# A fused attention and FFN kernel on one core: seven block products for the last pieces, and maxima sent through DRAM

## The chip, the cores and the metric

The kernel runs on one core of one Trainium2 chip. The metric is the device time of one execution in microseconds, 985.25 before the change (median of three runs, 983.32 to 985.38). TensorE (PE) multiplies, VectorE (DVE) and ScalarE (ACT) work element by element, GpSimd (POOL) clears memory here, and SyncE (SP) issues all transfers.

## The reference

`q`, `k` and `v` have 8 batches, 8 heads, 576 positions and 64 dimensions. Attention is causal by blocks of 64: a query sees every key of its own and of earlier blocks. The result, 4608 tokens of 512 numbers, goes through an FFN of 2048 hidden units:

```python
scores = scale * np.matmul(q, k.transpose(0, 1, 3, 2))     # scale = 1/8
scores = np.where(block_i >= block_j, scores, -1e9)
attn = softmax(scores)
x = (attn @ v), heads side by side                          # 4608 x 512
h = x @ w_in                                                # 512 x 2048
g = h * np.clip(h + 3.0, 0.0, 6.0) / 6.0
out = (g @ w_out).astype(np.float32)                        # 2048 x 512
```

## The kernel before

**Precision.** Most products are made of 16-bit numbers: each operand is scaled by a power of two and split into a high and a low half (`hi` and `lo`), and a product is three: hi·hi, hi·lo, lo·hi. The scale comes from the largest magnitude in the operand. For the weights it is taken by chunk of 256 hidden units (`NCH` = 8 chunks, `w_max`, line 678), for `v` by batch (`v_max`, 747). `pow2_scale` (561) turns maxima by partition, `mx`, into one maximum known to all 128 partitions. With `exact` it does so on TensorE: a product with the identity lays the 128 maxima side by side (`mt`), DVE reduces them, a second product with ones spreads the result (`mb`).

**Attention.** 32 slots, each a batch and a pair of heads (`n`). A slot's `q` and `k` are loaded, scaled and transposed by a DMA (`qk_load`, `qk_prep`, tile `qkT`). `s_group` (1035) makes scores (`s`), the softmax in `p` and the split `ph` or `phl`, which DMAs transpose into `pT`; `pv_group` (1157) multiplies by `v`, split by `v_prep` (761), and writes the slot's part of `x`, high and low half. The first four slots have versions in f32 (names with 32).

**The FFN.** The tokens are cut into 13 pieces (`pieces`, 1141): piece 0, 2 and 4 to 12 of 384 tokens, 1 and 3 of 192. Four buffers `xb` hold `x` of a piece by its number modulo 4. For each of 16 tiles of 128 hidden units, `f`, `ffn1_` (1246) makes `h` = 24 products of 64 hidden units by 384 tokens (4 depths of 128, 3 splits, 2 halves of the columns of the array, which run at the same time) in a PSUM tile `h`; then ScalarE makes `r` = relu(h + 3), DVE `r` = min(r, 6)·h, ScalarE or DVE the high half of `g`, DVE the low one. `ffn2_` (1302) accumulates `g` times `w_out` in three PSUM tiles `o`, 18 products of 512 columns for each `f`; after the last `f` they are scaled into tiles `osb` and stored. `g` has four buffers (`NGB`), `stage` (shared by `r`, `osb` and the preparation of weights) four, `raw` one.

**What sets the order.** Nothing is issued when it is written. The class `Recorder` (85) keeps every instruction with its tiles, a key (the time when it is wanted) and the engines that may do it (`scaled`, 150: "A", "V" or "P"). `schedule` (289) then plays the program on a model of the engines: whenever an engine is free it takes the ready instruction with the lowest key. Keys come from the times at the top: `AT` for the attention slots, `FT` for the pieces, `W0`, `S0`, `M0` for loads, splits and maxima of the weights; `ADV` makes TensorE's attention work earlier. A buffer is given out only if it doesn't block an instruction that stands earlier in the program (`room`, 335): where a tag has one buffer, an earlier user that hasn't begun holds back a later one. `QUEUE` (98) says when a transfer lands by the plan. The resulting order is emitted, instruction by instruction, each engine in its own fixed order; on the chip an engine waits for semaphores.

`ffn_step` (1361) gives the program order of the FFN: `ffn1` of the next tile, `ffn2` three tiles behind (`LAG`). `step` (1469) calls it at the piece's times once the piece's `x` is complete.

Of the kernel before, what the change touches and what calls it, by code (L numbers as in the profile page):

```python
# [24 lines left out]

U = 1.592
AS = (6.899, 12.918, 18.225, 24.115)
AL = 17.759
PV0 = 2.584
TA, TR, PR = 2.701, 5.502, 1.15  # L30
QR = 2.616
PVA, PVB = 1.013, 0.991
PHS = 18
# [4 lines left out]
EVR = 3  # L38
EVP = 4
PRO = True  # L40
MEM = 0

NMIN = 64
QL = -3.431
VL = -2.484
W0, WD = 16.803, 2.29
S0, SD = 55.334, 4.109
M0, MD = 36.221, 7.195
RT = (29.488, 39.58, 49.409, 59.423)
RS, RL, VL1 = 2.209, 24.843, 24.11  # L50
VM0, VMX = 49.529, 0.186
AT = ((4, 86.25), (6, 123.23), (8, 163.76), (9, 178.32), (10, 200.46), (12, 251.25), (14, 297.48), (15, 319.97), (16, 344.82), (24, 581.69), (32, 825.86))
FT = ((0, 34), (1, 120), (2, 165.28), (3, 233.86), (4, 274.28), (5, 355.06), (7, 504.5), (10, 755.22), (13, 989.58))
UNI = False
QP = 0.558
VP = 0.387
BLK = 64
# [23 lines left out]

ADV = {("tensor", "a"): 99.24}


class Recorder:
# [11 lines left out]
    LOADS = 95.0  # L97
    BIAS = {"vector": 250.0, "gpsimd": 500.0}
    EDGE = 0.0
    BURST, PATIENCE = 3, 4000.0  # L100

    def __init__(self, nc):
        self.nc = nc
        self.ops = []
        self.key = 0.0
        self.cls = ""
        self.joint = None
        self.adv = ADV
        for n in self.NAMES:
# [6 lines left out]
    def box(a):  # L116
        sz = mybir.dt.size(a.dtype)
# [58 lines left out]
    def add(self, ways):  # L176
# [318 lines left out]
def kernel(  # L495
# [50 lines left out]
    attp = ctx.enter_context(tc.tile_pool(name="att", bufs=2))  # L546
    ffp = ctx.enter_context(tc.tile_pool(name="ff", bufs=3))
    ps_s = ctx.enter_context(tc.tile_pool(name="ps_s", bufs=3, space=bass.MemoryType.PSUM))
    ps_h = ctx.enter_context(tc.tile_pool(name="ps_h", bufs=2, space=bass.MemoryType.PSUM))
# [10 lines left out]

    def pow2_scale(mx, n, nm, to=None, exact=False):
# [8 lines left out]
        if exact:  # L570
            pt_ = ps_s.tile([P, 512], F32, tag="s", name=f"mt_{nm}")
            nc.joint = "mt", nm
            for h in range(2):
                wide = mx[:, h % n:h % n + 1].to_broadcast([P, BLK])
                nc.tensor.matmul(pt_[h * BLK:(h + 1) * BLK, :P], wide, ident, start=True, stop=True)
            nc.joint = None
            dg = sm.tile([P, n + 1], F32, tag=f"dg{n}", name=f"dg_{nm}")
            nc.vector.tensor_reduce(dg[:, n:], pt_[:, :P], axis=AX.X, op=ALU.max)
            nc.vector.tensor_scalar_mul(dg[:, :n], ident[:, :(n - 1) * BLK + 1:BLK], dg[:, n:])
            mx = dg[:, :n]  # L580
        ps = ps_s.tile([P, 512], F32, tag="s", name=f"mb_{nm}")
        nc.joint = "mb", nm
        for h in range(2):
            nc.tensor.matmul(ps[h * BLK:(h + 1) * BLK, :n], ones[:, :BLK], mx, start=True, stop=True)
        nc.joint = None
        nc.vector.tensor_scalar_max(am, ps[:, :n], TINY)
# [52 lines left out]
    def w_load(w, c, half):  # L639
# [36 lines left out]
        )  # L676

    def w_max(c):

        acc = sm.tile([P, 2, 2], F32, tag="wacc", bufs=2, name=f"wacc{c}")  # L680
        for wi, w in enumerate("io"):
            for half in range(2):
                c32 = w_f32(w, c, half)
                ab = ffp.tile([P, WC], F32, tag="stage", bufs=NST_B, name=f"ab{w}{c}_{half}")
                ab = ab.rearrange("p (r l n) -> p r l n", r=c32.shape[1], l=2)
                nc.scalar.activation(ab, c32, AF.Abs, accum_out=acc[:, wi, half:half + 1])
        m = sm.tile([P, 2], F32, tag="wm", name=f"wm{c}")
        nc.vector.tensor_reduce(m, acc, axis=AX.X, op=ALU.max)
        pow2_scale(m, 2, f"w{c}", (pwio[:, c], rsio[:, c]), exact=True)

    def w_split(c):

        rs = rsio[:, c]
        for wi, w in enumerate("io"):
            for half in range(2):
                c32 = w_f32(w, c, half)
                part = w_part(w, c, half)
                hi, lo = (part[:, :, i].rearrange("p r (l n) -> p r l n", l=2) for i in range(2))
                nc.scaled(hi, c32, rs[:, wi:wi + 1], "AVP")
                nc.vector.scalar_tensor_tensor(  # L700
                    lo, c32, rs[:, wi:wi + 1], hi, op0=ALU.mult, op1=ALU.subtract
                )

# [43 lines left out]
    def v_max(n):  # L747
# [8 lines left out]
        if hp == NPAIR - 1:  # L756
            m1 = sm.tile([P, 1], F32, tag="vm1", name=f"vm1_{b}")
            nc.vector.tensor_reduce(m1, vmax[b], axis=AX.X, op=ALU.max)
            vscale[b] = pow2_scale(m1, 1, f"v{b}", exact=True)

# [11 lines left out]

    def h_scale(b):

        if b not in hs:
            t = sm.tile([P, NCH], F32, tag="sh", bufs=3, name=f"sh{b}")
# [3 lines left out]
            nc.vector.tensor_scalar_mul(t, t, C_H)  # L780
            hs[b] = t
        return hs[b]

# [373 lines left out]
    def pv_group(n, g):  # L1157
# [56 lines left out]
    gt = {}  # L1214
    acc = {}

    def spans(pc):
# [28 lines left out]
    def ffn1_(pc, f):  # L1246
        if pc == 0:
            return ffn1_f32(f)
        x, w, fc = xb[pc % 4], width(pc), f * P % NH
        ps = ps_h.tile([P, TP], F32, tag="h", name=f"h{pc}_{f}")  # L1250
# [51 lines left out]
    def ffn2_(pc, f):  # L1302
# [34 lines left out]
        for t, a in enumerate(acc.pop(pc)):  # L1337
            n, half = min(w - t * P, P), w - t * P < P
            o = ffp.tile([P, DM], F32, tag="stage", bufs=NST_B, name=f"osb{pc}_{t}")
            oc = o[:, :DM // 2] if half else o  # L1340
            ac = a[:, :DM // 2] if half else a
            nc.scaled(oc, ac, so[:, t:t + 1] if pc else 1.0 / 6.0, "AV")
            rows = out[row + t * P:row + t * P + n]
            if half:
# [183 lines left out]
```

## Time and profile before

| | before |
|---|---|
| median of 3 runs | 985.25 us (983.32 to 985.38) |
| the profiled execution | 982.83 us, span 981.0 |
| TensorE, matmul | busy 964.2 us (98%) |
| VectorE | 756.4 us (77%) |
| ScalarE | 696.5 us (71%) |
| granted TensorE clock | 0.999 |

The span runs from the first to the last instruction; the execution's time has 1.8 us more. In the profile, an instruction is named by engine, operation and tiles: `h<-x,win` is a product that writes tile `h`. All of them stand under line 491, where the planner emits, so tiles tell them apart. "<-" behind a time names what ended the wait. A product of one half of the array's columns is written 128*64.

### The profile page before, as it was taken

The page shows a single profiled execution, that of the slowest core. Times are in us where ns is not written, and L with a number is a line of the kernel's source. Part 1 is how long each engine was busy: PE and PEld are TensorE (multiplying, and loading weights), DVE is VectorE, ACT ScalarE, POOL GpSimd, SP SyncE. Part 2 cuts the span into 40 slices and gives each one's busy share as a digit, 9 for nine tenths or more (in the row PEclk, how much of TensorE's full clock was granted, in tenths as well). Part 3 has the DMA queues.
Part 4 walks back from the last instruction along what each step waited for, and adds up shares of the span by engine and source line. Part 5 has one row for each costly group of instructions (what it writes and reads, how often), then busy time and mean ns, then how long its engine had stood idle before and what let it go on. Part 6 is the DMA issues. An engine that isn't in the chain of part 4 may idle for free.

```text
span 981.0 us, 29087 instructions
## 1 busy us (share of the span) xinstructions
PE 964.2 (98%) x11754; PEld 722.9 (74%) x11754; DVE 756.4 (77%) x2081; ACT 696.5 (71%) x1840; POOL 28.3 (3%) x109
## 2 busy tenths in 40 slices
PE   8999999999999999999999999999999999999998
PEld 6655447877778867777777677777777777777776
DVE  6889998999989999999999898899886432332331
ACT  6899789778778888888878788787775433333332
POOL 3012000000000000000000000000000000000000
PEclk9999999999999999999999999999999999999999
DMA  6966689899898899898899898786664200000000
GB/s 141 277 204 223 159 154 178 169 183 189 155 173 148 149 175 157 170 162 148 161 186 177 151 188 156 132 164 131 108 133 77 36 34 1 1 33 1 34 2 33
DMA packets 414199, 128.91 MB, mean 131 GB/s; under 512 B 403184, under 2 KB 403440, under 8 KB 414064
## 3 DMA queue, kind: packets, MB, share of 16 engines
q1 hardware_dynamic: 414064, 127.05, 66.5%
q8 instruction: 92, 1.51, 0.6%
q14 instruction: 43, 0.35, 0.1%
HBM read 45.09 MB, written 9.44 MB: 56 GB/s over the span
## 4 chain that ended last, share of the span: by engine, by line
PE 58%; DVE 6%; DMA 2%; ACT 1%; issue 1%; DVEq 0%; ACTq 0%
PE o L491 25%; PE h L491 25%; PE s L491 4%; PE pv L491 4%; DMA pT<-ph 2%; DVE st L491 1%; DVE phl L491 1%; DVE ph L491 1%; DVE r L491 1%; DVE g L491 1%; DVE qks L491 1%; DVE vhl L491 0%; ACT p L491 0%; DVE x L491 0%; ACT r L491 0%
## 5 line engine op out<-in xcount | busy, mean ns | idle before, releaser
L491 PE MATMUL h<-x,win 128*64 128x384 f16 (+3 forms) x4790 | 440.7, 319 | 4.4 <-DVE r L491 4.4
L491 PE MATMUL o<-wout,g 128*64 128x512 f16 (+2 forms) x3424 | 432.3, 383 | 0.0
L491 PEld LDWEIGHTS <-win 128*64 128x64 f16 x4608 | 296.1, 110 | 62.5 <-issue 6.5
L491 PEld LDWEIGHTS <-g 128*64 128x64 f16 x3264 | 219.2, 110 | 91.6
L491 ACT ACTIVATE r<-h,eg,sh 128x192 f32<-128x192 f32 (+1 forms) x240 | 134.1, 580 | 115.2 <-PE h L491 110.8
L491 DVE SCALAR_TENSOR_TENSOR r<-r,eg,h 128x384 f32<-128x384 f32 (+1 forms) x192 | 110.3, 575 | 132.0 <-ACT r L491 131.3
L491 ACT ACTIVATE p<-s,st,esc 128x64 f32<-128x64 f32 (+1 forms) x280 | 163.1, 586 | 13.6 <-DVE ph L491 7.3
L491 DVE SCALAR_TENSOR_TENSOR g<-r,g 128x384 f16<-128x384 f32 (+1 forms) x192 | 99.5, 519 | 34.1 <-ACT g L491 33.3
L491 DVE TENSOR_REDUCE st<-s 128x1 f32<-128x64 f32 (+1 forms) x280 | 119.2, 446 | 6.9 <-PE s L491 6.1
L491 ACT ACTIVATE g<-r 128x384 f16<-128x384 f32 (+1 forms) x157 | 77.4, 494 | 59.2 <-DVE r L491 58.7
L491 PE MATMUL s<-qkT 128*64 128x64 f16 (+7 forms) x1120 | 101.8, 287 | 1.9 <-ACT p L491 1.3
L491 PEld LDWEIGHTS <-vhl 128*64 128x64 f16 x1680 | 74.0, 110 | 13.5 <-issue 4.1
L491 PEld LDWEIGHTS <-qkT 128*64 128x64 f16 x1120 | 62.0, 110 | 23.5 <-issue 7.6
L491 PE MATMUL pv<-pT,vhl 128*64 128x192 f16 (+2 forms) x1680 | 74.4, 233 | 1.9 <-DMA pT<-ph 0.9
L491 DVE SCALAR_TENSOR_TENSOR ph<-p,st,ph 128x256 f16<-128x256 f32 (+2 forms) x168 | 66.5, 444 | 0.1
L491 DVE SCALAR_TENSOR_TENSOR phl<-p,st,phl 128x512 f16<-128x512 f32 (+1 forms) x84 | 62.8, 789 | 0.3 <-ACT phl L491 0.3
L491 ACT ACTIVATE st<-st,esc 128x1 f32<-128x1 f32 (+2 forms) x127 | 36.8, 291 | 34.3 <-DVE st L491 32.9
L491 ACT ACTIVATION_READ_ACCUMULATOR p<-s,st,esc 128x1 f32 x280 | 55.0, 196 | 0.0
L491 ACT ACTIVATE ph<-p,st 128x64 f16<-128x64 f32 (+5 forms) x106 | 43.2, 450 | 15.8 <-DVE st L491 14.2
L491 DVE SCALAR_TENSOR_TENSOR qks<-qk,rs_q,qks 128x576 f16<-128x576 f32 x56 | 44.5, 807 | 0.1
L491 ACT ACTIVATE qks<-qk 128x576 bf16<-128x576 f32 x56 | 37.8, 677 | 0.3 <-DMA qkT<-qks 0.3
L491 ACT ACTIVATE x<-pv 128x192 f16<-128x192 f32 (+1 forms) x56 | 20.3, 363 | 11.5 <-PE pv L491 10.0
(150 smaller groups left out, 847.0 us busy)
## 6 DMA issues: line engine op xcount, KB each, us to landing
out_dram<-osb SPq DMA_DIRECT2D x35, 256.0 KB, 2.7
vnat<-in_v_dram SPq DMA_DIRECT2D x64, 128.0 KB, 3.0
qk<-in_q_dram SPq DMA_DIRECT2D x28, 288.0 KB, 3.4
qk<-in_k_dram SPq DMA_DIRECT2D x28, 288.0 KB, 4.3
rawi<-in_moe_w_in_dram SPq DMA_DIRECT2D x8, 512.0 KB, 4.5
rawo<-in_moe_w_out_dram SPq DMA_DIRECT2D x8, 512.0 KB, 4.7
ph<-in_moe_w_in_dram SPq DMA_DIRECT2D x6, 512.0 KB, 4.8
ph<-in_moe_w_out_dram SPq DMA_DIRECT2D x6, 512.0 KB, 4.0
```

Source lines behind the costliest of these rows:

```text
L491: getattr(eng, method)(*args, **kw)
```

## The change

Four things.

1. **Seven block products.** For pieces 10, 11 and 12 (`SW` = 10) `ffn1_seven` replaces `ffn1_`. It takes a chunk of 256 hidden units at once. The product is seen as 2 x 2 blocks of the weights (256 depths by 128 units) times 2 x 2 blocks of `x` (256 depths by 192 tokens), and is made by seven products of blocks and additions in place of eight products. The operands are sums of blocks: of weights, made by `w_forms` once for each chunk, and of `x`, by `x_forms` for each piece, each sum in f32 and split anew into `hi` and `lo`. The sums of weights are kept in buffers of attention (`homes`: tags `qkT`, `pT2`, `p`), those of `x` in `qk`, `qks` and `pT01`. All eight `w_forms` stand in the program ahead of piece 10's first product. The additions of the results are DVE's, into `hh`. For these pieces `pv_group` writes `x` once, in f32. They start only when all attention stands behind them in the program (`step`).
2. **Maxima as DRAM rows.** With `far` (weights from chunk 3, `v` from batch 1) `pow2_scale` stores the maxima by partition as rows in DRAM and loads them back broadcast to all partitions; DVE reduces them. Both transfers are SP's. `ROW` adds 5 us to the planned landing of the store and 2.5 us to that of the load.
3. **Wider steps.** `w_max` and `w_split` work on whole chunks, not halves. The first two tiles of `osb` get the `raw` buffer instead of `stage`; the very last tile is evicted and stored in two halves, by two queues.
4. **New planner times**: `U`, `AS`, `AL`, `QR`, `RT`, `AT`, `FT`, `ADV` and others.

The diff, without most new times and without the renaming that the third point needs:

```diff
-U = 1.592
-AS = (6.899, 12.918, 18.225, 24.115)
+U = 0.627
+AS = (6.363, 13.445, 20.163, 24.432)
...
+WFAR, VFAR = 3, 1
+SW = 10
+WF0, WFD = 769.667, 21.108
+XFA = 12.408
...
-AT = (..., (24, 581.69), (32, 825.86))
-FT = (..., (5, 355.06), (7, 504.5), (10, 755.22), (13, 989.58))
+AT = (..., (24, 564.98), (32, 785.9))
+FT = (..., (5, 349.28), (6, 400.48), (7, 495.43), (10, 765.43), (11, 833.3), (13, 966.06))
-ADV = {("tensor", "a"): 99.24}
+ADV = {("tensor", "a"): 53.22}
...
+        if exact and far:
+            row = drp.tile([n, P], F32, tag=f"row{n}", name=f"dr_row_{nm}")
+            nc.sync.dma_start(row.rearrange("n p -> p n"), mx)
+            al = sm.tile([P, n, P], F32, tag="al", bufs=1, name=f"al_{nm}")
+            nc.sync.dma_start(
+                al.rearrange("p n x -> p (n x)"),
+                row.rearrange("n p -> (n p)").rearrange("(o x) -> o x", o=1).to_broadcast([P, n * P]),
+            )
+            nc.vector.tensor_reduce(am, al, axis=AX.X, op=ALU.max)
+            nc.vector.tensor_scalar_max(am, am, TINY)
...
@@ pv_group
+            if pc >= SW:
+                nc.scaled(x_whole(pc)[:, hp, xs], ps[:, t0:t1], E_X / 4, "AV")
+                continue
...
+    homes = [("qkT", 3)] + [("pT2", 3)] + [("p", 1)] * 4 + [("qkT", 3)] + [("pT2", 3)]
+    def w_forms(c):
+        was, nc.key, nc.cls = (nc.key, nc.cls), WF0 + c * WFD, "w"
+        w32 = ffp.tile([P, NDT, NH], F32, tag="raw", bufs=1, name=f"w32_{c}")
+        nc.vector.tensor_add(w32, win[:, c, :, 0], win[:, c, :, 1])
+        a11, a12, a21, a22 = (w32[:, 2 * d:2 * d + 2, l * P:(l + 1) * P] for l in range(2) for d in range(2))
...
+        for i in range(2):
...
+            s = ffp.tile([P, 2, 2, P], F32, tag="stage", bufs=NST_B, name=f"ws{c}_{i}")
+            if not i:
+                nc.vector.tensor_add(s[:, 0], a21, a22)
+                nc.vector.tensor_sub(s[:, 1], s[:, 0], a11)
+            else:
+                nc.vector.tensor_sub(s[:, 0], a11, a21)
+                nc.vector.tensor_sub(s[:, 1], a12, last[:, 1])
...
+            nc.scaled(o[:, :, 0], s2, 1.0, "AV")
+            nc.vector.tensor_sub(o[:, :, 1], s2, o[:, :, 0])
...
+    def x_forms(pc):
+        was, nc.key = nc.key, line(FT, pc) - XFA
...
+        for r, b in ((r0, b11), (r1, x[:, 2:])):
+            nc.scaled(r[:, 0], b, 1.0, "AV")
+            nc.vector.tensor_sub(r[:, 1], b, r[:, 0])
...
+        for k in range(4):
...
+            nc.vector.tensor_sub(t, a, b)
+            nc.scaled(tt[:, k, 0], t, 1.0, "AV")
+            nc.vector.tensor_sub(tt[:, k, 1], t, tt[:, k, 0])
...
+    def ffn1_seven(pc, c):
+        if not wf:
+            for k in range(NCH):
+                w_forms(k)
+        if pc not in xform:
+            x_forms(pc)
...
+        def mul(o, w, x, nm):
+            for d in range(2):
+                for i, (wl, xl) in enumerate(((0, 0), (0, 1), (1, 0))):
+                    for h in range(2):
+                        r = slice(h * BLK, (h + 1) * BLK)
+                        nc.tensor.matmul(o[r], w[d][wl][:, r], x[d][xl], ...)
+        one_ = ps_h.tile([P, HP], F32, tag="h", name=f"u{pc}_{c}")
+        mul(one_, w11, x11, 1)
+        nc.scaled(hh[:, 5], one_, 1.0, "AV")
+        for k, runs in enumerate((
+            ((w12, x21, 2), (s2, t2, 6)), ((s1, t1, 5), (s3, t3, 7)), ((s4, x22, 3), (w22, t4, 4)),
+        )):
+            ps = ps_s.tile([P, 2, HP], F32, tag="s", name=f"u{pc}_{c}_{k}")
+            for j, run in enumerate(runs):
+                mul(ps[:, j], *run)
+            if k < 2:
+                with_ = hh[:, 5 - k].rearrange("p (o n) -> p o n", o=1).to_broadcast([P, 2, HP])
+                nc.vector.tensor_add((hh[:, 0:5:4], hh[:, 1:3])[k], ps, with_)
+                if k:
+                    nc.vector.tensor_add(hh[:, 3], ps[:, 0], hh[:, 2])
+            else:
+                nc.vector.tensor_add(hh[:, 1:3], ps, hh[:, 1:3])
...
@@ ffn2_
+            if t == 0:
+                pair = ffp.tile([P, 2, DM], F32, tag="raw", bufs=1, name=f"osb{pc}")
+            o = pair[:, t] if t < 2 else ffp.tile([P, DM], F32, tag="stage", bufs=NST_B, name=f"osb{pc}_{t}")
...
@@ ffn_step
+            while done1 >= SW * NFT and not done1 % 2 and done2 < done1 + 2 - NGB:
+                ffn2(*divmod(done2, NFT))
+                done2 += 1
...
@@ step
-        while owed and done1 < TOT and not left[done1 // NFT]:
+        while owed and done1 < TOT and not left[done1 // NFT] and (done1 < SW * NFT or not sum(left)):
```

After the additions a chunk goes on as before: for each of its two tiles of hidden units `r`, `g` and the second product.

More of the change, by code (lines that the diff above doesn't have):

```diff
@@ L97 @@
     LOADS = 95.0
[L98 removed]
+    ROW = 5000.0, 2500.0
     EDGE = 0.0
@@ L116, in box @@
     def box(a):
+        if not Recorder.on_chip(a):
+            return 0, 1, 0, 1
         sz = mybir.dt.size(a.dtype)
@@ L230, in queue @@
         lead, tail, rate = self.QUEUE[kind]
+        for a, more in zip(args, self.ROW):
+            if a.tensor.name.startswith("dr_"):
+                tail += more
         return lead, tail, nb / rate
@@ L580, in pow2_scale @@
[L580 to L586, printed above, removed]
+            nc.vector.tensor_scalar_max(am, ps[:, :n], TINY)
         nc.vector.tensor_scalar(
@@ L676, in w_load, with w_whole @@
         )
+    def w_whole(w, c):
+        if w == "i":
+            part = win[:, c]
+            c32 = win[:, c + 1].bitcast(F32) if c + 1 < NCH else None
+        else:
+            part = wout[:, 2 * c:2 * c + 2]
+            c32 = wout[:, 2 * c + 2:2 * c + 4].bitcast(F32) if c + 1 < NCH else None
+        if c32 is None:
+            t = flat(xb[2 if w == "i" else 3], F32)[:, :2 * WC]
+            c32 = t.rearrange("p (r l n) -> p r l n", r=part.shape[1], l=2)
+        return c32, part
     def w_max(c):
-        acc = sm.tile([P, 2, 2], F32, tag="wacc", bufs=2, name=f"wacc{c}")
+        acc = sm.tile([P, 2], F32, tag="wm", name=f"wm{c}")
         for wi, w in enumerate("io"):
[L682 to L689, printed above, removed]
+            c32, _ = w_whole(w, c)
+            ab = ffp.tile([P, WC], F32, tag="stage", bufs=NST_B, name=f"ab{w}{c}")
+            ab = ab.bitcast(BF16).rearrange("p (r l n) -> p r l n", r=c32.shape[1], l=2)
+            nc.scalar.activation(ab, c32, AF.Abs, accum_out=acc[:, wi:wi + 1])
+        pow2_scale(acc, 2, f"w{c}", (pwio[:, c], rsio[:, c]), exact=True, far=c >= WFAR)
     def w_split(c):
@@ L694, in w_split @@
         for wi, w in enumerate("io"):
[L695 to L702, printed above, removed]
+            c32, part = w_whole(w, c)
+            hi, lo = (part[:, :, i].rearrange("p r (l n) -> p r l n", l=2) for i in range(2))
+            nc.scaled(hi, c32, rs[:, wi:wi + 1], "AV")
+            nc.vector.scalar_tensor_tensor(
+                lo, c32, rs[:, wi:wi + 1], hi, op0=ALU.mult, op1=ALU.subtract
+            )
     gs = []
@@ L771, with h_scale @@
     hs = {}
-    def h_scale(b):
-        if b not in hs:
-            t = sm.tile([P, NCH], F32, tag="sh", bufs=3, name=f"sh{b}")
+    def h_scale(b, times=1.0):
+        if (b, times) not in hs:
+            t = sm.tile([P, NCH], F32, tag="sh", bufs=4, name=f"sh{b}_{int(times)}")
             nc.vector.scalar_tensor_tensor(
@@ L1215, with x_whole @@
     acc = {}
+    HP = TP // 2
+    wf = {}
+    xform = {}
+    homes = [("qkT", 3)] + [("pT2", 3)] + [("p", 1)] * 4 + [("qkT", 3)] + [("pT2", 3)]
+    room = []
+    def x_whole(pc):
+        return flat(xb[pc % 4], F32).rearrange("p (d n) -> p d n", d=NDT)
+    def w_forms(c):
[3 more added lines that the diff above has]
+        a11, a12, a21, a22 = (w32[:, 2 * d:2 * d + 2, l * P:(l + 1) * P] for l in range(2) for d in range(2))
+        wf[c] = []
+        last = None
+        for i in range(2):
+            if not room:
+                tag, n = homes.pop(0)
+                bufs = NPB if tag == "p" else 2
+                t = attp.tile([P, n, 2, 2, 2 * P], F16, tag=tag, bufs=bufs, name=f"wf{c}_{i}")
+                room.extend(t[:, j] for j in range(n))
+            o = room.pop(0)
+            s = ffp.tile([P, 2, 2, P], F32, tag="stage", bufs=NST_B, name=f"ws{c}_{i}")
+            if not i:
+                nc.vector.tensor_add(s[:, 0], a21, a22)
+                nc.vector.tensor_sub(s[:, 1], s[:, 0], a11)
+            else:
+                nc.vector.tensor_sub(s[:, 0], a11, a21)
+                nc.vector.tensor_sub(s[:, 1], a12, last[:, 1])
+            last = s
+            s2 = s.rearrange("p k d x -> p k (d x)")
+            nc.scaled(o[:, :, 0], s2, 1.0, "AV")
+            nc.vector.tensor_sub(o[:, :, 1], s2, o[:, :, 0])
+            wf[c] += [
+                [[o[:, k, l, d * P:(d + 1) * P] for l in range(2)] for d in range(2)] for k in range(2)
+            ]
+        nc.key, nc.cls = was
@@ new lines, in ffn1_seven @@
+    def ffn1_seven(pc, c):
[4 more added lines that the diff above has]
+            x_forms(pc)
+        x11, x21, x22, t1, t2, t3, t4 = xform[pc]
+        s1, s2, s3, s4 = wf[c]
+        w11, w12, w22 = (
+            [[win[:, c, 2 * h + d, l, f * P:(f + 1) * P] for l in range(2)] for d in range(2)]
+            for f, h in ((0, 0), (0, 1), (1, 1))
+        )
+        hh = (flat(xb[1], F32)[:, :6 * HP], ph01[1].rearrange("p l u x -> p (l u x)").bitcast(F32))[c % 2]
+        hh = hh.rearrange("p (k n) -> p k n", k=6)
+        def mul(o, w, x, nm):
+            for d in range(2):
+                nc.joint = "u", pc, c, nm, d
+                for i, (wl, xl) in enumerate(((0, 0), (0, 1), (1, 0))):
+                    for h in range(2):
+                        r = slice(h * BLK, (h + 1) * BLK)
+                        nc.tensor.matmul(
+                            o[r], w[d][wl][:, r], x[d][xl],
+                            start=d == 0 and i == 0, stop=d == 1 and i == 2,
+                        )
+            nc.joint = None
+        one_ = ps_h.tile([P, HP], F32, tag="h", name=f"u{pc}_{c}")
[12 more added lines that the diff above has]
+                    nc.vector.tensor_add(hh[:, 3], ps[:, 0], hh[:, 2])
+            else:
+                nc.vector.tensor_add(hh[:, 1:3], ps, hh[:, 1:3])
+        eg = g_scales()[0]
+        for l in range(2):
+            r = ffp.tile([P, TP], F32, tag="stage", bufs=NST_B, name=f"r{pc}_{2 * c + l}")
+            h = hh[:, 2 * l:2 * l + 2].rearrange("p k n -> p (k n)")
+            for b, c0, c1 in spans(pc):
+                nc.scalar.activation(
+                    r[:, c0:c1], h[:, c0:c1], AF.Relu,
+                    bias=eg[:, 1, c:c + 1], scale=h_scale(b, 4.0)[:, c:c + 1],
+                )
+            nc.vector.scalar_tensor_tensor(r, r, eg[:, 2, c:c + 1], h, op0=ALU.min, op1=ALU.mult)
+            g = ffp.tile([P, 2, TP], F16, tag="g", bufs=NGB, name=f"g{pc}_{2 * c + l}")
+            nc.scaled(g[:, 0], r, 4 * E_G, "AV")
+            nc.vector.scalar_tensor_tensor(
+                g[:, 1], r, 4 * E_G, g[:, 0], op0=ALU.mult, op1=ALU.subtract
+            )
+            gt[pc, 2 * c + l] = g
@@ L1248, in ffn1_ @@
             return ffn1_f32(f)
+        if pc >= SW:
+            return None if f % 2 else ffn1_seven(pc, f // 2)
         x, w, fc = xb[pc % 4], width(pc), f * P % NH
@@ L1338, in ffn2_ @@
             n, half = min(w - t * P, P), w - t * P < P
-            o = ffp.tile([P, DM], F32, tag="stage", bufs=NST_B, name=f"osb{pc}_{t}")
+            if t == 0:
+                pair = ffp.tile([P, 2, DM], F32, tag="raw", bufs=1, name=f"osb{pc}")
+            o = pair[:, t] if t < 2 else ffp.tile([P, DM], F32, tag="stage", bufs=NST_B, name=f"osb{pc}_{t}")
             oc = o[:, :DM // 2] if half else o
             ac = a[:, :DM // 2] if half else a
+            rows = out[row + t * P:row + t * P + n]
+            if pc == NPC - 1 and t == nt - 1:
+                for h, e in enumerate((nc.sync, nc.scalar)):
+                    cs = slice(h * DM // 2, (h + 1) * DM // 2)
+                    nc.scaled(o[:, cs], a[:, cs], so[:, t:t + 1], "AV")
+                    e.dma_start(rows[:, cs], o[:, cs])
+                continue
             nc.scaled(oc, ac, so[:, t:t + 1] if pc else 1.0 / 6.0, "AV")
-            rows = out[row + t * P:row + t * P + n]
             if half:
```

96 lines of the change are left out of this document (60 added, 36 removed).

## The prediction

> **What bounds the kernel now.** I read the page from the top: busy times, then the chain that ended last.
>
> ```profile
> span 981.0 us, 29087 instructions
> PE 964.2 (98%) x11754; PEld 722.9 (74%) x11754; DVE 756.4 (77%) x2081; ACT 696.5 (71%) x1840; POOL 28.3 (3%) x109
> DVE  6889998999989999999999898899886432332331
> PE 58%; DVE 6%; DMA 2%; ACT 1%; issue 1%; DVEq 0%; ACTq 0%
> ```
>
> TensorE is busy 98% of the span, but a busy PE need not run at its peak, so the rate has to be seen. DVE's digits give two regimes: eights and nines to about 740 us (attention beside the products of the FFN), then threes (the FFN alone). The end of the chain in order of time shows the second.
>
> ```profile
> 951.96 1.95 PE h L491 x24
> 953.91 1.94 PE o L491 x18
> 955.85 1.95 PE h L491 x24
> ```
>
> The 24 `h` instructions (12 pairs of column halves, 384 columns wide) take 1.95 us, the 18 `o` instructions (9 pairs, 512 wide) 1.94: 162.5 and 215.6 ns a pair. Two widths give a law: (215.6 - 162.5) / 128 = 0.415 ns a column, and 3.2 ns fixed. There is no gap between the three rows; no other engine sets this stage, and a pair taken away there is time gained. How a pair of 192 columns fares is seen elsewhere, in a timeline of TensorE (start, length; last row: the weight loads from the groups by form, with the mean length of one, 110 ns):
>
> ```profile
> 286.31 0.41 PE L491 MATMUL mt_v<-ident,vm 128*64 128x128 f32 x4
> 286.52 1.17 PE L491 MATMUL o<-wout,g 128*64 128x512 f16 x12
> 287.50 0.26 PE L491 MATMUL mb_v<-dg_v,one 128*64 128x1 f32 x4
> 287.59 1.19 PE L491 MATMUL h<-x,win 128*64 128x192 f16 x24
> 288.58 1.17 PE L491 MATMUL o<-wout,g 128*64 128x512 f16 x12
> ...
> 289.80 0.54 PE L491 MATMUL s<-qkT 128*64 128x64 f16 x12
> 290.14 0.94 PE L491 MATMUL h<-x,win 128*64 128x192 f16 x18
> L491 PEld LDWEIGHTS <-win 128*64 128x64 f16 x4608 | 296.1, 110 | 62.5 <-issue 6.5
> ```
>
> From start to start, 12 pairs of 192 columns took 288.58 - 287.59 = 0.99 us, 82.5 ns a pair; the law says 82.9.
>
> **The seven block products** (`ffn1_seven`). A chunk of 256 hidden units cost 2 x 12 pairs of 162.5 ns = 3.90 us. Now it is 7 products x 2 depths x 3 splits = 42 pairs of 192 columns: 42 x 82.9 = 3.48. The gain is 0.42 us a chunk, over 8 chunks and 3 pieces 10.0 us. All three pieces lie in the stage shown above.
>
> Here a rule speaks against the change. The Trainium skill ("TensorE: Matmul & The Clock Gate", section "LDWEIGHTS (loading the stationary operand)") puts a load at columns / 1.2 ns whatever the depth. By an estimate from that page, two loads of 64 columns one after the other take 107 ns, more than a pair's stream, and the 42 pairs would cost 4.5 us instead of 3.48; the sum would then hold +14 in place of -10 us. The trace disagrees: 24 loads and products fitted into 0.99 us, and the 12 of 64 columns into 290.14 - 289.80 = 0.34 us, 57 ns a pair, so the loads of the two halves overlap.
>
> **The maxima as DRAM rows** (`far`). Each old maximum held TensorE from 286.31 to 286.52 and from 287.50 to 287.59: 0.30 us. Twelve go (chunks 3 to 7, batches 1 to 7): 3.6 us, in stretches where TensorE is full. On DVE a reduction from PSUM and a small multiply go, a reduction of 128 or 256 SBUF columns comes: nothing either way. SP gets 24 more DMAs; the second of each two waits for the first to land.
>
> ```profile
> L491 PE MATMUL mt_v<-ident,vm x32: 272/273/323, 25.2 to 659.3; 128*64 128x128 f32 x32
> L491 PE MATMUL mb_v<-dg_v,one x32: 167/197/217, 26.9 to 664.8; 128*64 128x1 f32 x32
> out_dram<-osb SPq DMA_DIRECT2D x35, 256.0 KB, 2.7
> vnat<-in_v_dram SPq DMA_DIRECT2D x64, 128.0 KB, 3.0
> SPq L491 <- DVE ph L491: 94.0, 40, 7.8
> ```
>
> By these landings the way through DRAM takes about 2.7 + 3.0 = 5.7 us. The old way already took 664.8 - 659.3 = 5.5 us in the last batch, so the answer comes no later than it could before. Held behind SP's wait are the loads and the transposes of `pT` and `qkT`, for whose landing TensorE's `pv` and `s` wait. SP already waits 94 us in 40 places for `ph` alone, and the planner counts 5.0 and 2.5 us more for a row's landing, so other issues come between. No row shows a write of 4 bytes per partition; bounds 0 (covered) to 2.7 us for each of 12, once on the path. I take 0.
>
> **The output staging.** The tiles of a finished piece used the `stage` buffers; two of three now have `raw`.
>
> ```profile
> 293.07 0.51 ACT L491 ACTIVATE r<-h,eg,sh 128x192 f32<-128x192 f32 x1 [3.84 <-DMA out_dram<-osb]
> 293.61 0.41 DVE L491 SCALAR_TENSOR_TENSOR r<-r,eg,h 128x192 f32<-128x192 f32 x1 [3.14 <-ACT r L491]
> 294.08 1.18 PE L491 MATMUL h<-x,win 128*64 128x192 f16 x24 [2.03 <-DVE r L491]
> L491 ACT ACTIVATE osb<-o,so 128x512 f32<-128x512 f32 x27 | 17.5, 688 | 5.0 <-PE o L491 4.6
> L491 ACT ACTIVATE osb<-o,so 128x256 f32<-128x256 f32 x1 | 0.5, 472 | 0.0
> ```
>
> After piece 3 (two tiles, both now in `raw`) ScalarE waited 3.84 us for a store to free such a buffer, and TensorE 2.03 us behind it. I count -2.0 (bounds -2.0 to 0). At the very end the last eviction is halved over two engines and two queues: an eviction of 512 columns has 688 ns, of 256 columns 472, so -0.2.
>
> **ScalarE and DVE in the first phase.** Whole chunks instead of halves in `w_max` and `w_split` spare fixed costs, and the low half of `x` isn't written for pieces 10 to 12. TensorE is full there (first row; 21.88 of 25 in the second is the stretch with the stall above), so this alone is nothing:
>
> ```profile
> 75.00:100.00 25.00, 25.00 (x176) 13.10 (x177) 24.31 (x70) 23.60 (x60) 4.45 (x4) 1.00 0.68 212
> 275.00:300.00 25.00, 21.88 (x385) 18.15 (x382) 20.05 (x72) 19.69 (x56) 0.30 (x2) 1.00 0.94 166
> PE qt L491 <- DMA qf<-in_q_dram: 3.9, 1, 3.9
> ```
>
> The retuned times (`U`, `AS`, `RT`, `AT`, `FT`) put every queue into another order. No row prices that. All of TensorE's idle time is 981.0 - 964.2 = 16.8 us, 3.9 of it before the first load landed (last row, from the waits); a better order can win some 6 us, a worse one lose as much. I take 0.
>
> **The new work and where it must fit.** This term is the doubtful one. Prices:
>
> ```profile
> L491 DVE TENSOR_TENSOR x<-pf,rb 128x192 f32<-128x192 f32 x8 | 2.8, 355 | 0.9 <-PE pf L491 0.7
> L491 DVE SCALAR_TENSOR_TENSOR x<-pv,x 128x192 f16<-128x192 f32 x52 | 18.1, 350 | 1.2 <-PE pv L491 0.9
> L491 DVE SCALAR_TENSOR_TENSOR x<-pv,x 128x384 f16<-128x384 f32 x16 | 8.8, 548 | 0.6 <-PE mb_q L491 0.5
> L491 DVE SCALAR_TENSOR_TENSOR r<-r,eg,h 128x384 f32<-128x384 f32 x160 | 97.5, 609 | 127.2 <-ACT r L491 126.7
> L491 DVE SCALAR_TENSOR_TENSOR g<-r,g 128x384 f16<-128x384 f32 x160 | 88.5, 553 | 33.6 <-ACT g L491 32.8
> ```
>
> An addition of two tensors of 192 columns takes 355 ns, and a column more (548 - 350) / 192 = 1.03 ns. So, on DVE:
> - `w_forms`, a chunk: one of 1024 columns (1.21), four of 256 (0.42 each), two of 512 (0.685 each) = 4.26 us; eight are 34.1.
> - `x_forms`, a piece: nine of 384 (0.553 each) and one of 768 (0.95) = 5.9 us.
> - each chunk: adds of 384 three times and 192 once, 2.0 us, beside the old 2 x (0.609 + 0.553) = 2.3.
>
> A steady chunk needs 4.3 us of DVE in 3.48 + 3.89 = 7.4 us of TensorE: hidden. The start of piece 10 is another matter. In program order all eight `w_forms` come before the last second products of piece 9, and its output tiles need the `raw` buffer that `w_forms` uses; the planner gives it to them only after the eighth. Those tiles hold the accumulators of `o`, so piece 10's first second product waits for all eight, for `x_forms`, and for chunk 0. DVE's free time until that point (the numbers after the comma are busy time of PE, its weight loads, DVE, ScalarE, GpSimd; below them attention's last `s` and `pv`, and `osb`, the eviction of piece 9):
>
> ```profile
> 740.00:770.00 30.00, 29.58 (x366) 23.08 (x363) 19.62 (x49) 17.08 (x47) 0.00 (x0) 1.00 0.40 64
> 770.00:795.00 25.00, 25.00 (x291) 19.14 (x289) 7.30 (x13) 7.88 (x14) 0.00 (x0) 1.00 0.13 25
> 775.50:795.00 19.50, 19.50 (x214) 14.78 (x211) 5.51 (x10) 5.76 (x11) 0.00 (x0) 1.00 0.01 2
> 757.03 1.50 PE L491 MATMUL s<-qkT 128*64 128x512 f16 x16
> 774.22 1.28 PE L491 MATMUL pv<-pT,vhl 128*64 128x192 f16 x30
> L491 ACT ACTIVATE osb<-o,so x3: 687/687/687, 795.1 to 796.3; 128x512 f32<-128x512 f32 x3
> ```
>
> Free from 740 to 795: 30 - 19.6 and 25 - 7.3, together 28 us. The low halves that aren't written give 8 x (548 + 350) ns = 7.2 us more, so 35. Needed: 34.1 + 5.9 = 40, and 4.3 for each further chunk. Meanwhile TensorE can run two chunks of seven (`g` has four buffers), 7.0 us: 35 + 7 = 42 against 40 + 8.7 = 48.7. It lacks some 7 us if nothing else moves. It can lack nothing: TensorE can run up to six chunks before their results block, and neighbours on DVE overlap. Bounds 0 to 7; since attention's last times move 40 us forward (`AT` 825.86 to 785.9) while `FT` 10 moves 10 us back, I take the lower half, +2.5.
>
> **The sum**: -10.0 - 3.6 - 2.0 - 0.2 + 2.5 = -13.3. The profiled execution took 982.8 us (981.0 of span and 1.8 around it), so 969.5 by its scale. The three runs have a median of 985.25, 2.4 above it; I forecast **971**.
>
> **Rivals.**
> 1. *DVE sets the start of piece 10 outright*: all of the 7 us and some 3 more for `x_forms` of piece 11 are lost. For it: the budget above. Against: later times for FFN. 971 + 7.5 = 978.5.
> 2. *Slower: `w_forms` hardly begins before the last `pv`* at 774 to 775.5, because its target buffers (`qkT`, `pT2`, `p`) are attention's. Then only 19.5 - 5.5 = 14 us of DVE are free before 795, 5.9 for `x_forms` and 8.1 for 1.9 chunks. There remain 6.1 x 4.26 = 26 us, 12 of adds for six chunks and 4.6 for `r` and `g` of two: 43 us, in which TensorE has six chunks, 21 us. It stands 22 us: 971 - 2.5 + 22 = 990. It decides once more than some five `w_forms` are left at 775. Against it: the last `s` ends at 758.5, and a `qkT` comes free long before.
> 3. *The rows hold SP up*: seven waits of 2 us for batches reach `pv`: 971 + 14 = 985, no change. Against: 5.5 us was slack enough.
> 4. *Loads bind at 192 columns*: were a pair 110 ns, the mean of one load in the trace, 42 pairs take 4.62 us, 0.72 more than 3.90, times 24 = +17.3 in place of -10.0: 998. Against: the 82.5 ns above. (The rule of the Trainium skill cited above points this way.)
> 5. *The order gets better too*, by 6 to 8 us and no stall: 962.
>
> **Chances.** Forecast 60% (965 to 976), rival 1 17%, rival 2 7%, rival 3 5%, rival 4 2%, rival 5 9%. Less than 0.2%, 2 us, can't be told from no change here. Faster: the forecast, rivals 1 and 5, less an edge: 0.85; same 0.05 (rival 3); slower 0.10 (2, 4 and that edge). The range 961 to 982 takes in rivals 1 and 5.
>
> **What would show it.** The new first products at 82 to 84 ns a pair and 3.5 us a chunk; no idle time of TensorE before 800 us on `osb`; twelve fewer `mt` groups; waits of TensorE, if any, between the end of piece 9 and the first `o` of piece 10, released by `osb` or a `u` eviction, with DVE over 90% busy. A start of piece 10 with over 10 us of idle TensorE, pairs over 90 ns, or waits of `pv` for DMAs behind a row would make the forecast wrong.

## The result, and the profile after

The changed kernel takes **1015.54 us** (median of four runs, 1013.11 to 1018.76) where the kernel before took 984.51 beside it: 1.0318 times, with a 95% interval of 1.0283 to 1.0353. It is 31 us slower; the forecast was 971. The profiled execution took 1017.06 us. From its page, the span, the busy times, two rows of digits and the chain that ended last:

```profile
span 1015.3 us, 30760 instructions
PE 965.9 (95%) x12504; PEld 706.6 (70%) x12504; DVE 844.8 (83%) x2247; ACT 701.7 (69%) x1819; POOL 18.8 (2%) x101
PE   8996969988999998999999979999999999999998
PEclk9998989989999999999999999999999999999999
PE 28%; ACT 1%; DVE 0%; issue 0%
```

TensorE stands idle 1015.3 - 965.9 = 49.4 us, against 16.8 before. The idle time lies in the first two thirds of the digits, in attention. The last third is full; the seven products run in its second half, from 830 us on. The end of the chain in order of time (start, length):

```profile
963.53 3.47 PE u L502 x84
967.00 3.88 PE o L502 x36
970.88 3.46 PE u L502 x84
```

A chunk's first product is now 84 instructions, 42 pairs, in 3.46 us, 82.4 ns a pair, where before two times 1.95 us stood. So the tail became shorter by what was forecast, and some 45 us were lost elsewhere. The first trace of them is in the DMA issues (KB each, then median us from issue to landing, for those whose landing the profile shows):

```profile
out_dram<-osb SPq DMA_DIRECT2D x34, 256.0 KB, 3.4
...
qk<-in_q_dram SPq DMA_DIRECT2D x28, 288.0 KB, 5.5
...
dr_row_v<-vm SPq DMA_DIRECT2D x7, 0.5 KB, 7.6
dr_row_w<-wm SPq DMA_DIRECT2D x5, 1.0 KB, 9.5
```

The smallest transfers of the kernel, half a kilobyte, are among the slowest: 7.6 us, while the store of 256 KB takes 3.4. (A row of the weights holds two maxima per partition, so 256 pieces of 4 bytes where a row of `v` has 128.) The load of `qk` from `q` is slower too, 5.5 us against 3.4 before. SP's timeline around the row of batch 2, and below it the same slot's three transposes in the kernel before:

```profile
203.95 1.31 SPq L502 DMA_DIRECT2D dr_row_v<-vm  x1
205.31 1.13 SPq L502 DMA_DIRECT2D vnat<-in_v_dram  x2
206.48 0.67 SPq L502 DMA_DIRECT2D qk<-in_k_dram  x1
207.26 12.15 SPq L502 DMA_TRANSPOSE pT<-phl  x3
219.51 1.25 SPq L502 DMA_TRANSPOSE pT<-ph  x1
220.82 0.57 SPq L502 DMA_DIRECT2D al_v<-dr_row_v  x1
```

```profile
184.44 4.34 SPq L491 DMA_TRANSPOSE pT<-phl  x3
```

The three transposes behind the row's store take 12.15 us on SP instead of 4.34, and the row's load, planned behind them, goes out 17 us after the store. TensorE's waits in the changed kernel show what is late then (total us, times, longest); the last two rows, from the timeline, are waits of DVE (the bracket: idle before, and what ended it):

```profile
PE s L502 <- DVE pw_v L502: 8.0, 1, 8.0
...
PE mb_q L502 <- ACT p L502: 5.0, 1, 5.0
PE s L502 <- DMA qkT<-qks: 4.3, 2, 3.1
...
136.82 0.43 DVE L502 TENSOR_SCALAR sgo<-ph 128x512 uint32<-128x512 uint32 x1 [8.40 <-DMA ph<-in_moe_w_out_dram]
...
215.45 0.82 DVE L502 TENSOR_REDUCE vmax<-vnat 128x1 f32<-128x640 f32 x1 [5.13 <-DMA vnat<-in_v_dram]
```

The first two name other engines, but both go back to a late load. `pw_v` is a scale that comes from a row, but ahead of it DVE had stood 8.40 us for a load of weights, issued at 124.42, 1.9 us behind a row's store, and reached `pw_v` at 140 us. The 5.0 us end likewise after DVE's 5.13 us for a load of `vnat`, issued behind the store at 203.95. The third is a late transpose.

### The profile page after: what moved, and what is told of

Its sections match the earlier page's. It is cut to its first block, busy times and chain, and to the rows that moved or that the text cites. A ratio compares the mean times of both kernels' runs of the same rounds, so it can differ in the third digit from the quotient of the medians.

```text
span 1015.3 us, 30760 instructions
## 1 busy us (share of the span) xinstructions
PE 965.9 (95%) x12504; PEld 706.6 (70%) x12504; DVE 844.8 (83%) x2247; ACT 701.7 (69%) x1819; POOL 18.8 (2%) x101
## 5 line engine op out<-in xcount | busy, mean ns | idle before, releaser
L502 PE MATMUL o<-wout,g 128*64 128x512 f16 (+2 forms) x3412 | 422.2, 384 | 0.0
L502 PE MATMUL h<-x,win 128*64 128x384 f16 (+3 forms) x3644 | 335.9, 321 | 6.5 <-DVE g L502 3.7
L502 PEld LDWEIGHTS <-g 128*64 128x64 f16 x3264 | 211.8, 110 | 105.7 <-issue 0.2
L502 PEld LDWEIGHTS <-win 128*64 128x64 f16 x4320 | 245.9, 111 | 54.7 <-issue 4.5
L502 DVE TENSOR_REDUCE st<-s 128x1 f32<-128x64 f32 (+1 forms) x280 | 115.9, 445 | 7.7 <-PE s L502 7.3
L502 ACT ACTIVATE r<-h,eg,sh 128x192 f32<-128x192 f32 (+1 forms) x176 | 98.2, 578 | 31.5 <-PE h L502 28.9
L502 PE MATMUL s<-qkT 128*64 128x64 f16 (+7 forms) x1120 | 94.6, 292 | 17.1 <-DVE pw_v L502 8.0
L502 DVE SCALAR_TENSOR_TENSOR r<-r,eg,h 128x384 f32<-128x384 f32 (+1 forms) x144 | 80.5, 562 | 23.8 <-ACT r L502 23.4
L502 PEld LDWEIGHTS <-qkT 128*64 128x64 f16 x1120 | 57.6, 112 | 39.3 <-issue 17.9
L502 ACT ACTIVATE st<-st,esc 128x1 f32<-128x1 f32 (+2 forms) x124 | 35.4, 290 | 33.9 <-DVE st L502 33.1
L502 PEld LDWEIGHTS <-wf 128*64 128x64 f16 x1152 | 49.0, 110 | 0.9 <-DVE x L502 0.7
```

The costliest lines, as they stand in the source:

```text
L502: getattr(eng, method)(*args, **kw)
```

## The experiments

Three theories stood at the start. A: the 12 rows cost the time, and all other terms are as predicted. B: the new order (`AT`, `FT`, `RT` and so on) is worse by itself. C: the seven products or their preparation cost it. Within A, theory L says that the answer comes late and its readers wait, theory S that the store disturbs the DMAs around it. What was expected stands ahead of each result.

**All maxima on TensorE again.**

```diff
-WFAR, VFAR = 3, 1
+WFAR, VFAR = 8, 8
```

> The changed kernel with every maximum made on TensorE as before (WFAR = VFAR = 8): seven products, wider steps and new planner times stay. Theory A, the rows through DRAM cost the time (write at 203.95, answer at 226.9 us in the changed kernel, TensorE idle 5.0 us from 200 to 225): the loss of about 45 us goes and 968 to 976 us are left, TensorE idle under 25 us. Theory B, the new planner times made a bad order: still over 1000 us.

Measured: 973.17 us, 0.9859 [0.9826, 0.9892] of the kernel before. A stands, B and C fall: without the rows the change gains 14 us by the ratio, and the rows cost 1015.54 - 973.17 = 42 us (45 by the two ratios). Its page and some windows (after the comma busy us of TensorE, its weight loads, DVE, ScalarE, GpSimd; then granted clock, DMA share, GB/s):

```profile
span 971.7 us, 30951 instructions
PE 956.2 (98%) x12616; PEld 729.3 (75%) x12616; DVE 846.3 (87%) x2264; ACT 701.5 (72%) x1814; POOL 19.0 (2%) x101
```

```profile
75.00:150.00 75.00, 74.90 (x563) 40.52 (x563) 71.44 (x211) 58.39 (x132) 1.38 (x6) 1.00 0.68 161
375.00:400.00 25.00, 24.93 (x338) 19.53 (x336) 23.85 (x71) 20.53 (x54) 0.60 (x4) 1.00 0.99 144
475.00:500.00 25.00, 25.00 (x326) 19.62 (x324) 22.03 (x63) 17.43 (x45) 0.30 (x2) 1.00 0.70 141
575.00:600.00 25.00, 25.00 (x337) 19.93 (x334) 23.48 (x66) 19.66 (x52) 0.30 (x2) 1.00 0.84 156
```

The same windows of the changed kernel, in each of which a row is under way (the same clock times; after the first stall not quite the same work):

```profile
75.00:150.00 75.00, 58.98 (x317) 28.81 (x317) 51.95 (x138) 44.49 (x100) 1.22 (x6) 0.86 0.71 133
375.00:400.00 25.00, 20.84 (x277) 14.23 (x275) 19.83 (x56) 17.81 (x52) 0.30 (x2) 0.99 1.11 160
475.00:500.00 25.00, 21.89 (x270) 14.57 (x268) 18.44 (x55) 17.02 (x49) 0.15 (x1) 0.93 0.88 147
575.00:600.00 25.00, 19.90 (x252) 14.03 (x250) 16.53 (x49) 13.96 (x40) 0.30 (x2) 0.93 0.93 123
```

TensorE loses 16 us where most rows of the weights and the first of `v` fall, and 3 to 5 us at later rows; all other engines do less too, so none of them is the bound. Of the 43.6 us between the two spans 49.4 - 15.5 = 33.9 are idle time and 9.7 are longer busy time: the granted clock, 1.00 in every one of these windows without the rows, is 0.86 in the first of them with rows, 0.99, 0.93 and 0.93 in the others. How much of the loss is the clock and how much the waits was not separated.

**Half of the rows.** Only those of `v`, then only those of the weights:

```diff
-WFAR, VFAR = 3, 1
+WFAR, VFAR = 8, 1     (rows of v)
+WFAR, VFAR = 3, 8     (rows of the weights)
```

> Rows for v alone (batches 1 to 7), weights on TensorE. Theory A: the stalls of TensorE between 200 and 600 us stay, those from 75 to 150 us go; summed by TensorE's missing work in the changed kernel (about 22 us from 75 to 150, about 25 later) 992 to 1000 us. Theory B: over 1000.

> Rows for the weights alone (chunks 3 to 7), v on TensorE. Theory A: the stalls from 75 to 150 us stay, the later ones go: 988 to 998 us. Theory B: over 1000.

Measured: 1012.54 (1.0253 [1.0188, 1.0319]) and 1005.5 (1.0182 [1.014, 1.0224]), that is 39 and 32 us above the kernel without rows. Both lie above what theory A gave them, in the range of B, but the kernel without rows has the new times too and contradicts B. What fails is the assumption that the losses add up: each half alone costs most of what both cost (42). So the price isn't a fixed sum for each row. It may depend on what the planner places behind each, since that order differs between the three; this wasn't tested, and why the halves don't add up stays open.

**The seven products undone.** With rows, then without:

```diff
-SW = 10
+SW = 13
```

> The changed kernel without the seven products (SW = 13), rows and new planner times stay. If the seven products are worth the 10 us of the pairs of products they spare, and their additions are hidden, this takes about 1025 us; if they cost time (DVE 25.00 of 25 us busy from 775 to 825), 1015 or less.

> All maxima on TensorE and no seven products (WFAR = VFAR = 8, SW = 13): wider steps, other output staging and new planner times alone. The prediction's terms: 10.0 us for the seven products less a stall of 0 to 7, so 973.2 + 3 to 10 = 976 to 983 us. If the new planner times carry the gain: 973 or less.

Measured: with rows 1039.8 (1.053 [1.0486, 1.0573]), above both of the times expected; this mixes the products with another order around the rows and tells nothing of the products alone. Without rows 983.13, 0.9978 [0.9967, 0.9989] of the kernel before, at the upper end of what the prediction's terms give. The seven products are then worth 983.13 - 973.17 = 10.0 us (11.7 by the ratios).

**Late answer or disturbed DMAs.** The kernel without rows, with the same twelve stores added and nothing that reads them:

```diff
+            if exact and (nm[0] == "w" and int(nm[1:]) >= 3 or nm[0] == "v" and int(nm[1:]) >= 1):
+                row = drp.tile([n, P], F32, tag=f"row{n}", name=f"dr_row_{nm}")
+                nc.sync.dma_start(row.rearrange("n p -> p n"), mx)
```

> All maxima on TensorE, and beside them the same twelve stores of 4 bytes per partition to DRAM that the changed kernel makes; nothing reads them. Theory S (the store itself holds up the transfers issued behind it: loads behind a row landed after 9 to 12 us instead of 3 to 5): over 995 us, with stalls of TensorE at the same places. Theory L (the maxima only come late for those that wait for them): as without rows, 970 to 977.

Measured: 1044.16, 1.0587 [1.0556, 1.0618]: 71 us more than without the stores, 5.9 us for each, though nothing waits for them. L falls as the main cause; the store itself disturbs. Then both DMAs of a row on GpSimd's queue, and, in another kernel, the planner told of a later landing:

```diff
-            nc.sync.dma_start(row.rearrange("n p -> p n"), mx)
+            nc.gpsimd.dma_start(row.rearrange("n p -> p n"), mx)
...
-    ROW = 5000.0, 2500.0
+    ROW = 15000.0, 7500.0
```

> The changed kernel with both transfers of a row issued by GpSimd instead of SP; nothing left out. If what costs is the place of the slow store in SP's queue, with loads and transposes behind it: 972 to 985 us. If the DMA engines that both queues share are held up: 1000 to 1016.

> The changed kernel with the planner told that a row's store lands 15 us late and its load 7.5 (before 5 and 2.5), so that readers are put further behind. Theory L: most of the loss goes, 975 to 990 us. Theory S: the transfers behind the store are late all the same, 1000 us and more.

Measured: 1038.21 (1.0528 [1.0472, 1.0584]) and 1043.87 (1.0585 [1.0551, 1.062]). Neither SP's place in the order nor the planned distance is what costs: a row on another queue costs no less, even more than the 1000 to 1016 expected of shared engines. The Trainium skill ("DMA: Bandwidth & Descriptors", section "Issuing engines are not separate DMA queues") says that transfers issued from several engines share the same 16 DMA engines; the 1038 us agree.

**What in the store.** Four kernels gave the unread store another shape, from the constant `ident`:

```diff
+                row = drp.tile([P, P], F32, tag=f"row{n}", name=f"dr_row_{nm}")
+                nc.sync.dma_start(row, ident)          (512 bytes a partition)
...
+                nc.sync.dma_start(row, ident[:, :16])   (64 bytes)
+                nc.sync.dma_start(row, ident[:, :64])   (256 bytes)
+                nc.sync.dma_start(row, ident[:16, :1])  (4 bytes from 16 partitions)
```

> The same as the run with unread stores, but each store writes 512 bytes per partition (64 KB) instead of 4. If it is the size of the pieces that makes the store slow: 970 to 978 us. If any store to DRAM between the loads does: as with 4 bytes.

> No rows used; twelve unread stores of 64 bytes per partition, 128 pieces (with 512 bytes: 973.4 us, with 4: 1044.2). If only single words are slow: 972 to 977. If every piece below 512 bytes is: over 1000.

> The same with 256 bytes per partition. If the threshold lies at 512 bytes: over 1000 us; if 64 bytes are enough already: 972 to 977.

> The same with 4 bytes from each of 16 partitions, an eighth of the pieces. If the time goes by the number of small pieces, an eighth of 71 us: about 982. If a store of small pieces costs a fixed hold: 1030 and more. If 16 pieces go to 16 engines side by side: 973 to 977.

Measured: 973.41, 972.84, 969.71 and 975.13, all within some 4 us of the 973.17 without stores. But these runs don't tell the shape of the store from its moment: a constant is ready at once, so the planner sent all twelve out before 71 us, ahead of the stretch where the rows hurt. The next four therefore make the stored value from the maximum at its own time, by one DVE instruction, and differ in the store alone:

```diff
+                wide = sm.tile([P, P], F32, tag="al", bufs=1, name=f"al_{nm}")
+                nc.vector.tensor_scalar(wide, ident, mx[:, :1], 1.0, op0=ALU.mult, op1=ALU.mult)
+                row = drp.tile([P, P], F32, tag=f"row{n}", name=f"dr_row_{nm}")
+                nc.sync.dma_start(row, wide)                   (512 bytes a partition)
...
+                nc.sync.dma_start(row, wide[:, :16])            (row [P, 16]: 64 bytes)
+                nc.sync.dma_start(row[:, :1], wide[:, :1])      (row [P, P]: 4 bytes, 512 apart)
+                nc.sync.dma_start(row, wide[:, :1])             (row [P, 1]: 4 bytes, side by side)
```

> All maxima on TensorE. When the maxima of chunks 3 to 7 and batches 1 to 7 are there, DVE makes a tile from them (one more instruction of 128 columns) and SP stores 512 bytes per partition of it, unread. Theory S4 (4-byte pieces are what is slow, wherever they stand): 972 to 978 us. Theory T (any store at these moments is slow; the earlier unread stores from a constant went out before 71 us and so met no attention): over 1020.

> The same with 64 bytes per partition. S4 with a limit at 512 bytes: over 1000 us; single words alone slow: 972 to 978; theory T: over 1020.

> The same with 4 bytes per partition that land 512 bytes apart in DRAM. If the pieces are slow because all 128 fall into the same 512 bytes: 972 to 980 us. If 4-byte pieces are slow wherever they land (S4), or theory T: over 1020.

> The same with 4 bytes per partition side by side, 512 bytes in all, as the changed kernel stores them, from the new tile: the control. Every theory but chance: 1025 to 1045 us. If it is fast, the moment or the source made the difference, not the pieces.

Measured: 974.92 (0.9893 [0.9864, 0.9922]), 974.57 (0.989 [0.9861, 0.9918]), 975.36 (0.9898 [0.9869, 0.9926]) and **1023.93** (1.0391 [1.0348, 1.0433]). The last two are the decisive pair: the same 128 pieces of 4 bytes and the same instructions in the same order (in the records of TensorE 17 pairs of neighbouring matmuls, which start within nanoseconds of each other, stand the other way round); only the addresses in DRAM differ, 512 bytes apart or side by side. The control came 1 us under the range expected of it. From the page and the DMA issues, first apart, then side by side:

```profile
span 974.3 us, 30979 instructions
...
qk<-in_q_dram SPq DMA_DIRECT2D x28, 288.0 KB, 3.6
...
dr_row_v<-al_v SPq DMA_DIRECT2D x7, 0.5 KB, 3.7
```

```profile
span 1023.3 us, 30979 instructions
...
qk<-in_q_dram SPq DMA_DIRECT2D x28, 288.0 KB, 4.7
...
dr_row_v<-al_v SPq DMA_DIRECT2D x7, 0.5 KB, 6.5
```

(The 6.5 rests on one store whose landing the profile shows.) SP's timeline shows the same thing as in the changed kernel. Side by side, three transposes that follow a row's store:

```profile
486.60 0.57 SPq L502 DMA_DIRECT2D dr_row_v<-al_v  x1
487.28 1.62 SPq L502 DMA_DIRECT2D vnat<-in_v_dram  x3
489.00 9.27 SPq L502 DMA_TRANSPOSE pT<-phl  x3
```

The same row and the same transposes with the pieces apart take 4.11 us instead of 9.27:

```profile
451.46 0.57 SPq L502 DMA_DIRECT2D dr_row_v<-al_v  x1
452.13 1.63 SPq L502 DMA_DIRECT2D vnat<-in_v_dram  x3
454.09 4.11 SPq L502 DMA_TRANSPOSE pT<-phl  x3
```

So 48.6 us hang on where the 4-byte pieces fall. The size of a piece, the number of pieces, the moment, SP's order or a reader don't make the cost by themselves; 128 pieces of 4 bytes in the same 512 bytes of DRAM do.

The traces also keep the time of every DMA packet, and these show what is held up. The longest packet took 2.1 us in the kernel before, 2.3 without rows, 2.4 with the pieces apart, 2.5 with 64 or 512 bytes. Side by side, 147 packets took over 2.6 us, the longest 7.6; all of them began within 10 us after a row's store was issued, and none is a piece of 4 bytes: they belong to other transfers. The changed kernel has 83 such packets, the kernel with the rows on GpSimd's queue 126, of which 123 are in the queue of SP's transfers. Among the early unread stores only the one of 16 pieces of 4 bytes, side by side too, has any: nine, up to 3.1 us, with no loss of time that the runs could show. How many pieces in how narrow a stretch it takes was not tried further.

**The row kept, in few pieces.** DVE transposes the maxima in blocks of 32, so that four partitions hold 32 of them each, and the row is stored in four pieces of 128 bytes; it is read as before:

```diff
+            tr = sm.tile([P, n, 32], F32, tag=f"tr{n}", name=f"tr_{nm}")
+            for i in range(n):
+                nc.vector.transpose(tr[:, i], mx[:, i:i + 1].to_broadcast([P, 32]))
-            nc.sync.dma_start(row.rearrange("n p -> p n"), mx)
+            nc.sync.dma_start(row.rearrange("n (g x) -> g n x", x=32), tr[0:P:32])
```

> The changed kernel, rows through DRAM for the same twelve maxima, but DVE first transposes them in blocks of 32 (one or two more small instructions), so that a row is stored from 4 partitions in pieces of 128 bytes instead of from 128 partitions in pieces of 4; all else as changed. If the many small pieces side by side were the whole loss: 967 to 976 us, at or below the 973.2 with all maxima on TensorE. If pieces that share 512 bytes of DRAM are slow at any size, or the way through DRAM is late in itself: over 985.

Measured: **970.72 us** (970.02 to 971.96), 0.9852 [0.9832, 0.9871]. This is the whole change with one step mended, 1.5% below the kernel before. Four pieces in the same 512 bytes of DRAM are cheap, and no packet took over 2.2 us. From its page:

```profile
span 969.5 us, 30795 instructions
PE 952.1 (98%) x12518; PEld 703.7 (73%) x12518; DVE 848.1 (87%) x2267; ACT 696.8 (72%) x1816; POOL 19.0 (2%) x101
```

Against the kernel without rows TensorE is busy 4.1 us less and the span is 2.2 us shorter; the intervals of the two ratios overlap, so that this last gain isn't shown by the times.

## Why the prediction was wrong, step by step

**The step that failed** is the cost of the maxima as DRAM rows: "No row shows a write of 4 bytes per partition; bounds 0 (covered) to 2.7 us for each of 12 ... I take 0." Measured: 42 us by the kernel without rows (45 by the ratios), 3.5 to 3.7 a row, outside the upper bound. There were two faults in it. The price was taken from the nearest store, 256 KB in pieces of 2 KB, by bytes and landing; but the store in 4-byte pieces landed in 7.6 and 9.5 us (medians of the two kinds of row), not in 2.7. And the cost was counted once, as the row's own way to its reader. The kernel with unread stores shows that the transfers behind the store pay: 71 us with no reader at all. An upper bound should have been what SP and TensorE lose if every transfer behind a row waits for it.

**Rival 3** (rows hold SP up) pointed the right way but was priced at 14 us by waits of SP for a landing, and its mechanism was another: the rows cost no less on GpSimd's queue. It was set aside with "5.5 us was slack enough", which spoke of the answer's lateness only.

**The seven products**: predicted 82 to 84 ns a pair and -10.0 us. The chain shows 82.4 ns, the pair of kernels without rows 10.0 us. Right. The rule that loads of weights bind (rival 4; the Trainium skill, "TensorE: Matmul & The Clock Gate", section "LDWEIGHTS (loading the stationary operand)") would make it 107 ns a pair by an estimate from that page, were two loads to go one after the other; the 82.4 ns show that the loads of the two halves don't.

**Output staging and the end**: predicted -2.2. The kernel with neither rows nor seven products, which keeps these and the new order, stands at 983.13 against 985.66, -2.5. The stall after piece 3 is gone: TensorE is busy 24.68 us in the window where it had 21.88 of 25 (second row):

```profile
200.00:225.00 25.00, 22.63 (x301) 17.51 (x297) 22.88 (x71) 20.22 (x56) 0.30 (x2) 0.93 1.02 189
275.00:300.00 25.00, 24.68 (x422) 20.30 (x420) 22.87 (x78) 22.07 (x62) 0.30 (x2) 1.00 0.96 169
```

The first of these rows shows a small stall elsewhere, 22.63 us where the kernel before had 23.38, so the -2.5 is the sum of staging, end and order; the order's own share, taken as 0, was not measured apart.

**The start of piece 10**: the mechanism came as described, the size did not. In the changed kernel the `raw` buffer holds two output tiles of piece 9 back until 850.0 and later (the third has a `stage` buffer, and one eviction came at 837.7; second row), and DVE is busy 49.59 of 50 us (third row, columns as above). TensorE meanwhile ran chunks of seven products and stood 0.51 us:

```profile
847.86 1.18 PE L502 MATMUL u<-xt,wf 128*64 128x192 f16 x24 [0.51 <-DVE x L502]
```

```profile
L502 ACT ACTIVATE osb<-o,so x2: 669/678/687, 837.7 to 850.0; 128x512 f32<-128x512 f32 x2
```

```profile
800.00:850.00 50.00, 49.49 (x758) 40.23 (x754) 49.59 (x107) 26.73 (x59) 0.00 (x0) 1.00 0.20 40
```

So 0.5 in place of +2.5 (0.5 without rows too), and rivals 1 and 2 fall. The prices on DVE, by groups in the changed kernel (busy us, mean ns), were right to within 3%: predicted 1210, 420 and 685 ns:

```profile
L502 DVE TENSOR_TENSOR w<-win 128x1024 f32<-128x1024 f16 x8 | 9.7, 1211 | 0.0
L502 DVE TENSOR_TENSOR ws<-w 128x256 f32<-128x256 f32 x16 | 6.1, 409 | 0.0
L502 DVE TENSOR_TENSOR wf<-ws,wf 128x512 f16<-128x512 f32 x16 | 10.7, 676 | 0.0
```

**The maxima taken from TensorE**: predicted -3.6; 4.1 us less busy time where the rows are cheap. With all of it the kernel with the mended store stands at 970.7, 0.3 from the forecast of 971: the forecast was about right for a row that costs nothing. That it fits to 0.3 is in part luck: the start of piece 10 came 2 us cheaper than forecast, the time gained by the maxima isn't clear of the noise, and 971 was set between the two scales of the sum (969.5 by the profiled execution, 972 by the median of 985.25). For rows that cost something the prediction had rival 3 alone, with a chance of 0.05 and a price three times too small; its 0.10 for a slower kernel belonged to rivals 2 and 4.

## What to carry to other kernels

Price a transfer by what lands behind it, not only by its own way to its reader, and not by its bytes: where the trace shows nothing of its shape, the bound is all that is queued behind it. Values of one word per partition should not go side by side into a DRAM row as one store of 128 pieces; here it paid to gather them first (a DVE transpose of 32-blocks and four pieces of 128 bytes) or to leave them on TensorE, where a maximum cost 0.30 us. A saving of whole products in a stage that TensorE alone bounds came in full, because its preparation found room on DVE.

## What the runs showed of the hardware

- A store of 128 four-byte pieces to neighbouring DRAM addresses delays the DMAs behind it: 49 us over 12 stores with the pieces side by side (1023.93 us), nothing measurable with the same pieces 512 bytes apart (975.36) or with 64 or 512 bytes a piece (974.57, 974.92). The Trainium skill ("DMA: Bandwidth & Descriptors", section "Specifications") names 512 bytes as the least for full rate, with a read-modify-write below it; a piece below 512 bytes wasn't enough for the loss here. Many such writes close together, one after the other, would fit both, but what the DMA engines or the memory do inside is not shown by these traces.
- The delay reaches other queues: with the rows on GpSimd's queue the kernel took 1038.21 us, and 123 of its 126 packets over 2.6 us are in the queue of SP's transfers.
- The price of twelve such stores was 42, 49 and 71 us in kernels that differ in what is placed around them.
- In stretches with stalls of attention the granted clock was lower: 0.86, 0.93 and 0.93 in three windows of the changed kernel that had 1.00 without the rows (0.99 in a fourth). TensorE's busy time was 9.7 us longer; how much of it is the clock's was not separated.
